# Batch 0's exchange through DRAM, the offset behind the last DFT, and small constants off the head of a queue

## The chip, the cores and the metric

The kernel runs on one core of a Trainium2 chip. The metric is the device time of one execution in microseconds (us); lower is better. Each kernel was run several times and the median is quoted. A difference of more than 2% counts as faster or slower, anything less as the same. Where a number comes from a profile it belongs to one profiled execution, whose span is about 2 us shorter than the time of the same execution.

## The reference

Eight batches of 3008 tokens by 256 channels go through a spectral mix and then through an expert:

```python
X = np.fft.rfft(x, axis=1)                       # x: (8, 3008, 256)
Yr = X.real @ w_r - X.imag @ w_i + b_r
Yi = X.real @ w_i + X.imag @ w_r + b_i
Yr = sign(Yr) * max(|Yr| - 0.01, 0); Yi likewise # soft shrinkage
y  = np.fft.irfft(Yr + 1j * Yi, n=3008, axis=1)

h = y.reshape(24064, 256) @ w_in                 # w_in: (256, 2048)
r = max(h, 0)
out = (s * r * r + b) @ w_out                    # w_out: (2048, 256)
```

## The kernel before

A transform of 3008 = 94 x 32 points is done in two steps, so there is a first DFT (94 rows in, 96 out), a middle one of 32 points, and on the way back a middle inverse and a last DFT. The middle stages work on "pairs", 24 a batch. Between the first DFT and the middle, and between the middle and the last, the data changes its layout. Batches 1 to 7 do that through DRAM: `u` is written to `ud` and fetched as `us`; `v` is written to `vd` and fetched as `vs`. Their stages are strewn over the expert tiles of the batch before, one unit in this or that slot (a slot is one of the 16 column blocks of the first expert matmul; a tile of 512 tokens has 16 slots).

Batch 0 has nothing to hide behind. So it keeps everything in SBUF and turns the layout by matmuls with an identity matrix:

```python
def inv_dft(ec, u):
    ps = other_bank()
    z = zt.pop((ec, u))
    for j in range(4):
        nc.tensor.matmul(ps[:, j * P : (j + 1) * P], z[:, j, :], T_t[:, 4 * u + j, :], start=True, stop=True)
    evac(vt[:, ec, :, 16 * u : 16 * u + 16], ps.rearrange("p (k n) -> p n k", n=N2), 512)

def turn(ec, k):                                  # line 435
    ps = two_banks()
    for j in range(8):
        nc.tensor.matmul(ps[0:96, j // 4, (j % 4) * P : (j % 4) * P + P],
                         vt[:, ec, 8 * k + j, :], eye_t, start=True, stop=True)
    h, n = divmod(8 * k, HW)
    evac(vs[(0, h)][:, n : n + 8, ec * P : (ec + 1) * P], ps[0:96].rearrange(...), 1024)
```

(The profile calls the matmul engine, TensorE, PE, and its weight loads PEld; POOL is GpSimd and SP is SyncE, which both issue transfers.) `evac` copies PSUM to SBUF on VectorE (DVE) or ScalarE (ACT), whichever has less work. The schedule of what follows:

```python
more = first_batch()
schedule(0, 8, more)                              # rest of batch 1's first DFT
plan.setdefault(17, []).append(lambda: emit_load_x(2))
...                                               # cut: scaling of w_out, bias
schedule(14, 20, corr_units())                    # the offset that soft shrinkage adds, built on DVE
schedule(30, 42, s23_units(1))                    # middle stages of batch 1, slots 30 to 72
schedule(82, 12, s4_units(1))                     # last DFT of batch 1
```

Of the kernel before, what the change touches and what calls it, by code (L numbers as in the profile page):

```python
# [14 lines left out]
P = 128  # L15
# [57 lines left out]
def _offset_rows(inv):  # L73

    v = inv.reshape(2, 2, N2, NPAIR, 2, N2).sum(axis=2)
    return v.transpose(0, 1, 3, 4, 2).reshape(2, P, NPAIR)


def _tile_order(nb):


    tiles = []
    rest = []
    for b in range(nb):
        tiles += [("main", b, j, 512) for j in range(5)]
        pr, half = divmod(b, 2)
        if pr == 0:
            rest.append(("tail", 0, 448 * half, 448))
        elif half == 1:
            rest += [("tail", pr, 0, 512), ("tail", pr, 512, 384)]  # L90
        if rest:
            tiles.append(rest.pop(0))
    return tiles + rest


@with_exitstack
def kernel(
# [20 lines left out]
    YSCALE = 1.0 / (N * VSCALE)  # L118
# [4 lines left out]


    ones_r, ones_i = _offset_rows(inv)
    real_row = np.zeros((P, 1), bool)
    real_row[[0, 64]] = True
    assert np.abs(np.where(real_row, ones_i, ones_r)).max() < 1e-9
    O_d = nc.inline_tensor(
        np.where(real_row, ones_r, ones_i).astype(np.float32), name="offset_rows"  # L130
    ).ap()
    A_d = nc.inline_tensor(first.astype(np.float16), name="dft_first").ap()
    F_d = nc.inline_tensor(fwd.astype(np.float16), name="dft_fwd").ap()
    T_d = nc.inline_tensor(inv.astype(np.float16), name="dft_inv").ap()
    C_d = nc.inline_tensor(last.astype(np.float16), name="dft_last").ap()
# [4 lines left out]
    E_d = nc.inline_tensor(np.eye(P).astype(np.float16), name="identity").ap()  # L140
# [7 lines left out]
    xpool = ctx.enter_context(tc.tile_pool(name="xp", bufs=5))  # L148
    upool = ctx.enter_context(tc.tile_pool(name="up", bufs=2))
# [59 lines left out]
    F_c = uspool.tile([P, NPAIR, 2, N2], F16, name="F_c", tag="us")  # L209
    nc.sync.dma_start(out=F_c.rearrange("p q r k -> p q (r k)"), in_=F_d)  # L210
# [3 lines left out]
    for r in (0, 64):  # L214
        for i, bv in enumerate((b_r, b_i)):
            nc.sync.dma_start(out=b_g[r : r + 1, i], in_=bv.unsqueeze(0))
    b_h = cpool.tile([P, D], F16, name="b_h")
# [5 lines left out]
    eye_t = cpool.tile([P, P], F16, name="eye_t")  # L223
    nc.sync.dma_start(out=eye_t, in_=E_d)
# [8 lines left out]
    o_t = cpool.tile([P, NPAIR], F32, name="o_t")  # L233
    nc.sync.dma_start(out=o_t, in_=O_d)
    bl = cpool.tile([P, D], F32, name="bl")
    nc.sync.dma_start(out=bl, in_=b_i.unsqueeze(0).to_broadcast([P, D]))
    for r in (0, 64):
        nc.sync.dma_start(out=bl[r : r + 1], in_=b_r.unsqueeze(0))
# [6 lines left out]
    for dc in range(DC):  # L245

        nc.gpsimd.tensor_copy(out=w_in_t[dc][0:1, 0:1], in_=T_c[0:1, 0, 0:1])
        nc.gpsimd.dma_start(out=w_in_t[dc], in_=moe_w_in[dc * P : (dc + 1) * P, :])
# [21 lines left out]
    F_2 = [uspool.tile([P, H, P], F16, name="F_2", tag="us") for _ in range(2)]  # L270
    for f in F_2:
        nc.vector.memset(f, 0.0)

    nc.vector.memset(b_h, 0.0)
    nc.vector.tensor_copy(out=b_h[0:1], in_=b_g[0:1, 0])
    nc.vector.tensor_copy(out=b_h[64:65], in_=b_g[64:65, 1])
# [10 lines left out]
    def place_tables():  # L287
        for i in range(2):
            nc.scalar.copy(out=W_t[:, :, i], in_=w_st[i])
        for a in range(2):  # L290
            r = slice(64 * a, 64 * a + 64)
            nc.vector.tensor_copy(out=blocks(F_t)[r, :, :, a], in_=F_c[r])

            for h, f in enumerate(F_2):
                q = slice(h * H, h * H + H)
                nc.vector.tensor_scalar_mul(
                    out=blocks(f)[r, :, 0, a], in0=F_c[r, q, 1], scalar1=-1.0
                )
                nc.vector.tensor_copy(out=blocks(f)[r, :, 1, a], in_=F_c[r, q, 0])
        for i in range(4):  # L300
            r = slice(32 * i, 32 * i + 32)
            c = 64 * (i % 2)
            nc.scalar.copy(out=T_t[r, :, c : c + 64], in_=T_c[r])  # L303

    cs = []
    sq_last = [None]

    def scale_w_out(q):
        st = wo_st[q]
        if not cs:  # L310
            cs.append(other_bank())
        wb = zpool.tile([P, 2, D], F16, name="wb", tag="z")
        with tc.issue_after(sq_last[0].ins):
            nc.vector.tensor_scalar_mul(
                out=w_out_t[:, 2 * q : 2 * q + 2, :], in0=st, scalar1=s_bc
            )
            nc.vector.tensor_scalar_mul(out=wb, in0=st, scalar1=bb_bc)
        load["dve"] += 0.8
        for j in range(2):
            nc.tensor.matmul(  # L320
                cs[0][:, 0:D], ones, wb[:, j],
                start=(q == 0 and j == 0), stop=(q == MC // 2 - 1 and j == 1),
            )
# [8 lines left out]
    def first_batch():  # L332
# [20 lines left out]
        with tc.issue_after(last_dve.ins), tc.issue_after(last_act.ins):  # L353
            place_tables()
        emit_load_x(1)
        for q in range(MC // 2):
            emit_load_w_out(q)


        U = NPAIR // 4  # L360
        vt = bigpool.tile([P, DC, N2, 96], F16, name="vt", tag="corr")
        gs = {}
        zt = {}
        g_last = [None]

        def mix(ec, u):
            ps = two_banks().rearrange("p h (j r e) -> p (h j) r e", j=2, r=2)
            for j in range(4):
                q = 4 * u + j
                for dc in range(DC):  # L370
                    nc.tensor.matmul(
                        ps[:, j], ut[:, dc, 4 * q : 4 * q + 4, :],
                        W_t[:, dc, :, ec * P : (ec + 1) * P],
                        start=(dc == 0), stop=(dc == DC - 1),
                    )
            g = vpool.tile([P, 4, 2, P], F16, name="g0", tag="v")
            if u % 3 == 1:
                nc.scalar.copy(out=g, in_=ps)
                load["act"] += 1.02
            else:  # L380
                g_last[0] = nc.vector.tensor_tensor(
                    out=g, in0=ps,
                    in1=b_g[:, :, ec * P : (ec + 1) * P].unsqueeze(1).to_broadcast([P, 4, 2, P]),
                    op=ALU.add,
                )
                load["dve"] += 1.2
            gs[(ec, u)] = g

        def fwd_dft(ec, u):
            ps = one_bank().rearrange("p (j e) -> p j e", j=4)  # L390
            g = gs.pop((ec, u))
            seeded = u % 3 == 1
            if seeded:
                nc.tensor.matmul(
                    ps, sel_t,
                    b_h[:, ec * P : (ec + 1) * P].unsqueeze(1).to_broadcast([P, 4, P]),
                    start=True, stop=False, skip_group_check=True,
                )
            for j in range(4):
                q = 4 * u + j  # L400
                for r, f in enumerate((F_t[:, q, :], F_2[q // H][:, q % H, :])):
                    nc.tensor.matmul(
                        ps[:, j, :], f, g[:, j, r, :], start=(r == 0 and not seeded),
                        stop=(r == 1), skip_group_check=seeded,
                    )
            pos = mpool.tile([P, 4, P], F32, name="m", tag="m")
            nc.scalar.activation(out=pos, in_=ps, func=AF.Relu, bias=neg_lam)
            z = zpool.tile([P, 4, P], F16, name="z", tag="z")
# [5 lines left out]
            zt[(ec, u)] = z  # L414

        def inv_dft(ec, u):
            ps = other_bank()
            z = zt.pop((ec, u))
            for j in range(4):
                nc.tensor.matmul(  # L420
                    ps[:, j * P : (j + 1) * P], z[:, j, :], T_t[:, 4 * u + j, :],
                    start=True, stop=True,
                )
            evac(
                vt[:, ec, :, 16 * u : 16 * u + 16],
                ps.rearrange("p (k n) -> p n k", n=N2), 512,
            )

        for h in range(2):
            vs[(0, h)] = vspool.tile([96, HW, D], F16, name="vs", tag="vs")  # L430

        def turn(ec, k):
            ps = two_banks()
            for j in range(8):
                nc.tensor.matmul(
                    ps[0:96, j // 4, (j % 4) * P : (j % 4) * P + P],
                    vt[:, ec, 8 * k + j, :], eye_t, start=True, stop=True,
                )
            h, n = divmod(8 * k, HW)
            evac(  # L440
                vs[(0, h)][:, n : n + 8, ec * P : (ec + 1) * P],
                ps[0:96].rearrange("p h (j e) -> p (h j) e", e=P), 1024,
            )

        last = s4_units(0)
        more = s1_units(1)

        def some(n):
            for _ in range(n):
                if more:  # L450
                    more.pop(0)()

        steps = [(ec, u) for ec in range(DC) for u in range(U)]
        for i in range(2 * U + 2):
            if i < 2 * U:
                mix(*steps[i])
            if 0 <= i - 1 < 2 * U:
                fwd_dft(*steps[i - 1])
            if 0 <= i - 2 < 2 * U:
                inv_dft(*steps[i - 2])  # L460
            k = i - U - 2
            if 0 <= k < 4:
                turn(0, k)
            if 0 <= k - 1 < 4:
                last.pop(0)()
                last.pop(0)()
            if i >= 2 * U:
                some(3)
            if i == 6:
                with tc.issue_after(g_last[0].ins):  # L470
# [365 lines left out]
```

## Time and profile before

| | before |
|---|---|
| median of three runs | 900.83 us (899.37 to 901.06) |
| span of the profiled run | 900.1 us |
| mean granted clock of TensorE (share of full speed) | 0.991 |
| PE, DVE, ACT busy | 96%, 72%, 70% |
| first matmul of the expert stage (line 674) | 61.2 us |
| from there to the end | 838.9 us |

The last two rows: a *head* up to the first expert matmul and a *rest* behind it.

What the transfers do while the old exchange runs is in the windows of 5 us (after the window and its length come busy time and instructions of PE, its weight loads, DVE, ACT and POOL, then the granted clock, the share of the DMA engines, GB/s):

```profile
45.00:50.00 5.00, 4.33 (x67) 3.86 (x65) 4.77 (x8) 4.42 (x8) 0.00 (x0) 1.00 0.02 5
55.00:60.00 5.00, 3.73 (x49) 2.60 (x47) 2.75 (x4) 4.30 (x6) 0.51 (x1) 1.00 0.96 194
```

From 40 to 55 us the DMA engines are idle: the turns are on PE, and no transfer is on the path.

### The profile page before, as it was taken

The numbers are of one execution on the slowest core, as the hardware profiler recorded it, in microseconds if no ns is written. First come the engines' busy times: TensorE is split into PE (matmuls) and PEld (weight loads), VectorE is DVE, ScalarE is ACT, GpSimd is POOL, SyncE is SP. The second block draws the span as 40 slices with busy tenths as digits, with TensorE's granted clock in tenths as the row PEclk, the third lists the DMA queues.
The fourth block names the chain that finished last, engine by engine and source line by source line (L and its number), as shares of the span: only waits on it lengthen the run. The fifth ranks groups of instructions, "written<-read, shape, count | busy, mean of one in ns | idle before, by whom it ended". The sixth has DMA issues, their size and how long they took to land.

```text
span 900.1 us, 16484 instructions
## 1 busy us (share of the span) xinstructions
PE 861.8 (96%) x6748; PEld 610.8 (68%) x6748; DVE 652.4 (72%) x870; ACT 631.6 (70%) x785; POOL 33.2 (4%) x58
## 2 busy tenths in 40 slices
PE   2989998999999999999999999999999999999997
PEld 2756765767767676677767776777767777766665
DVE  4779776677678767777778677777767777676664
ACT  2879776667776677767776767777777676776662
POOL 2310000000000000000000000000000000000000
PEclk9989999899999999999999999999999999999999
DMA  8735146512365117612465115631254121411111
GB/s 183 188 75 148 47 109 154 148 33 59 86 184 129 57 48 185 178 36 60 88 181 131 57 36 139 163 92 54 65 155 132 36 62 47 118 41 36 36 36 53
DMA packets 81407, 86.91 MB, mean 97 GB/s; under 512 B 5422, under 2 KB 73268, under 8 KB 79988
## 3 DMA queue, kind: packets, MB, share of 16 engines
q1 hardware_dynamic: 76820, 70.39, 26.5%
q0 software_dynamic: 4512, 15.47, 10.3%
q8 instruction: 53, 0.87, 0.4%
q14 instruction: 22, 0.18, 0.1%
HBM read 52.55 MB, written 46.66 MB: 110 GB/s over the span
## 4 chain that ended last, share of the span: by engine, by line
PE 83%; ACT 6%; DMA 5%; DVE 4%; issue 1%; SPq 1%; DVEq 0%; ACTq 0%
PE psh L674 33%; PE psa L735 33%; PE psf L562 7%; PE psf L495 3%; ACT rt L681 2%; PE psf L633 2%; PE psf L544 2%; PE psf L580 2%; DMA ud<-u 2%; DMA T_c<-dft_inv 2%; DVE gt L688 1%; DMA vs<-vd 1%; ACT T_t L303 1%; DVE m L568 1%; ACT gt L685 1%
## 5 line engine op out<-in xcount | busy, mean ns | idle before, releaser
L681 ACT ACTIVATE rt<-psh 128x1024 f32<-128x1024 f32 (+2 forms) x384 | 385.4, 1005 | 176.4 <-PE psh L674 175.4
L735 PE MATMUL psa<-w_out_t,gt 128*128 128x256 f16 x3024 | 456.3, 273 | 0.0
L688 DVE TENSOR_TENSOR gt<-rt 128x1024 f16<-128x1024 f32 (+2 forms) x291 | 348.6, 1199 | 134.4 <-ACT rt L681 133.2
L735 PEld LDWEIGHTS <-gt 128*128 128x128 f16 x3024 | 295.4, 98 | 191.5 <-issue 7.0
L674 PE MATMUL psh<-yt,w_in 128*128 128x512 f16 x1280 | 382.0, 380 | 0.5 <-DVE yt L175 0.3
L674 PEld LDWEIGHTS <-w_in 128*128 128x128 f16 x1536 | 143.8, 98 | 26.8 <-issue 3.4
L685 ACT ACTIVATE gt<-rt 128x1024 f16<-128x1024 f32 (+1 forms) x93 | 98.1, 1055 | 2.5
L562 PE MATMUL psf<-W_t,xf 128*128 128x256 f16 x672 | 87.2, 273 | 0.0
L170 ACT CAST u<-psf 96x512 f16<-96x512 f32 x99 | 57.0, 578 | 26.6 <-PE psf L495 24.8
L748 DVE TENSOR_TENSOR ost<-psa,bias_bc 128x512 f32<-128x512 f32 (+2 forms) x98 | 65.1, 666 | 11.8 <-PE psa L735 8.8
L562 PEld LDWEIGHTS <-xf 128*128 128x128 f16 x672 | 65.5, 98 | 8.9 <-issue 0.4
L674 PE MATMUL psh<-tail,w_in 128*128 128x384 f16 (+2 forms) x256 | 70.3, 356 | 0.0
L568 DVE TENSOR_TENSOR m<-psf,lamb 128x512 f32<-128x512 f32 x84 | 57.6, 686 | 9.7 <-PE psf L562 9.7
L587 DVE TENSOR_TENSOR v<-psf,corr 128x512 f16<-128x512 f32 x84 | 57.0, 682 | 6.9 <-PE psf L580 6.8
L570 DVE SCALAR_TENSOR_TENSOR z<-psf,m 128x512 f16<-128x512 f32 x84 | 58.0, 690 | 2.5
L170 ACT CAST xf<-psf 128x512 f16<-128x512 f32 x84 | 48.7, 579 | 13.2 <-PE psf L544 13.1
L171 ACT ACTIVATE yt<-psf 128x480 f16<-128x480 f32 (+2 forms) x73 | 37.7, 536 | 16.2 <-PE psf L633 16.0
L495 PE MATMUL psf<-x,A_t 94*96 94x512 f16 x112 | 44.2, 394 | 3.7 <-DVE z L570 1.4
L550 DVE TENSOR_SCALAR xf<-xf 128x256 f16<-128x256 f16 x84 | 18.2, 222 | 36.5 <-ACT xf L170 36.5
L633 PE MATMUL psf<-C_t,vs 96*128 96x96 f16 x480 | 37.2, 209 | 7.2 <-DMA vs<-vd 4.3
L633 PEld LDWEIGHTS <-vs 96*128 96x128 f16 x512 | 33.1, 100 | 12.1 <-DMA vs<-vd 4.6
L194 POOL DMA_DIRECT2D x<-in_x_dram x32 | 16.7, 524 | 480.4 <-PE psf L495 471.0
(66 smaller groups left out, 343.0 us busy)
## 6 DMA issues: line engine op xcount, KB each, us to landing
out_dram<-ost SPq DMA_DIRECT2D x160, 128.0 KB
x<-in_x_dram POOLq DMA_DIRECT2D x32, 376.0 KB, 6.2
ud<-u SPq DMA_DIRECT2D x28, 384.0 KB
us<-ud SPq DMA_DIRECT2D x28, 384.0 KB
vd<-v SPq DMA_DIRECT2D x42, 256.0 KB
vs<-vd SPq DMA_DIRECT2D x14, 768.0 KB
wo_st<-in_moe_w_out_dram POOLq DMA_DIRECT2D x8, 256.0 KB, 4.8
out_dram<-ost SPq DMA_DIRECT2D x16, 112.0 KB
```

The costliest lines, as they stand in the source:

```text
L170: return None, nc.scalar.copy(out=dst, in_=src)
L495: nc.tensor.matmul(ps[0:96, :], A_t[0:N1, :], x16[(b, c)][0:N1, j * D : (j + 2) * D], start=True, stop=True,)
L562: nc.tensor.matmul(ps[:, j, :], xt[:, j * DC + dc, lo : lo + P], W_t[:, dc, w], start=(m == 0 and dc == 0), stop=(m == 1 and dc == DC - 1),)
L568: nc.vector.tensor_tensor(out=m, in0=ps, in1=lamb, op=ALU.max)
L570: nc.vector.scalar_tensor_tensor(out=z, in0=ps, scalar=2 * LAM, in1=m, op0=ALU.add, op1=ALU.min)
L633: nc.tensor.matmul(ps[:, j * 96 : (j + 1) * 96], vs[(b, h)][:, k, ec * P : (ec + 1) * P], C_t, start=True, stop=True,)
L674: nc.tensor.matmul(o, w_in_t[dc][:, mc * P : (mc + 1) * P], r, start=(dc == 0), stop=(dc == DC - 1),)
L681: nc.scalar.activation(out=rt[:, :, 0:w], in_=ps[:, :, 0:w], func=AF.Relu)
L685: nc.scalar.activation(out=gt[:, :, 0:w], in_=rt[:, :, 0:w], func=AF.Square)
L688: sq_last[0] = nc.vector.tensor_tensor(out=gt[:, :, 0:w], in0=rt[:, :, 0:w], in1=rt[:, :, 0:w], op=ALU.mult)
L735: nc.tensor.matmul(ps[0:n, h, :], gts[(ti, mc // 2)][:, mc % 2, sub * P : sub * P + n], w_out_t[:, mc, :], start=(mc == 0), stop=(mc == MC ...
L748: nc.vector.tensor_tensor(out=ost[0:m, lo:hi], in0=ps[0:m, lo:hi], in1=bias_bc[0:m, lo:hi], op=ALU.add,)
```

## The change

Four intents. Batch 0's exchange goes through DRAM as in the other batches, in groups of pairs while the mix runs, so that 64 matmuls and 8 large evictions go. The casts of the bias and the placing of the table T_t move on DVE behind the first eviction of the mix, and the loads of the bias ahead of a large table, so that nothing waits at DVE's head. The offset is added as one signal behind the last DFT, in place of a `corr` tile added to every `v`. And the middle stages of batch 1 run earlier.

```diff
+    vd = dpool.tile([NPAIR, P, D], F16, name="vd", tag="vd")
+    vd_rows = vd.rearrange("q (k n) e -> (q k) n e", n=N2)
 ...
-    def turn(ec, k): ...                     # 64 matmuls with the identity, 8 evictions
+        def inv_dft(i):
+            ...                              # two matmuls of 256 columns
+            v = xfpool.tile([P, 2 * DC * 192], F16, name="v0", tag="xf")   # three buffers
+            v = v[:, 0 : 2 * D].rearrange("p (j e) -> p j e", j=2)
+            evac(v, ps, 512)
+            nc.sync.dma_start(out=vd[2 * i : 2 * i + 2].rearrange("q p e -> p q e"), in_=v)
+        def fetch(k0, k1):
+            for h in range(2):
+                last[1] = nc.gpsimd.dma_start(
+                    out=vs[(0, h)][k0:k1], in_=vd_rows[k0:k1, h * HW : (h + 1) * HW, :])
 ...                                         # cut: the loop over i = 0 to 13, whose last lines are
+            if i in (5, 9):
+                fetch(8 * (i - 5), 8 * (i - 1))
+        fetch(64, 96)
+        with tc.issue_after(last[1].ins):
+            emit_load_raw()                  # w_out once more, for the bias: 2 MB read
+        for u in s1_units(1, True):          # first DFT of batch 1, all 16 units
+            u()
 ...
+    def place_t():                           # called behind the first eviction of the mix, on DVE
+        nc.vector.tensor_copy(out=b_h[0:1], in_=b_g[0:1, 0])
+        nc.vector.tensor_copy(out=b_h[64:65], in_=b_g[64:65, 1])
+        for i in range(4): ...               # T_t, was nc.scalar.copy
 ...
-            nc.vector.tensor_tensor(out=v[...], in0=ps, in1=corr[0][...], op=ALU.add)
+            evac(v[:, h : h + 2, :], ps, 512)
 ...
+            nc.vector.scalar_tensor_tensor(  # last DFT of batches 1 to 7
+                out=yt[:, ec, n2 : n2 + w, :], in0=off[0][:, n2 : n2 + w, :],
+                scalar=bl[:, 1, ec : ec + 1], in1=ps[...], op0=ALU.mult, op1=ALU.add)
 ...
-    schedule(30, 42, s23_units(1))
+    schedule(16, 44, s23_units(1))
+    plan.setdefault(17, []).append(emit_load_next)   # x of batch 2
+    plan.setdefault(30, []).append(emit_load_off)    # 1.5 MB, the offset signal
```

Also: four x buffers for five, three `u` buffers for two, loads of x of batch 1 and w_out behind a gate (an instruction that waits for earlier data and that the loads have to follow), the scale of the last DFT in its table, and tiles of another shape ("wide") for batches 0 and 1.

## The prediction

> **What bounds the kernel now.** I read the page first, parts 1 and 2.
>
> ```profile
> PE 861.8 (96%) x6748; PEld 610.8 (68%) x6748; DVE 652.4 (72%) x870; ACT 631.6 (70%) x785; POOL 33.2 (4%) x58
> PE   2989998999999999999999999999999999999997
> PEclk9989999899999999999999999999999999999999
> ```
>
> PE is busy nearly always, so I asked whether busy means full. By-shape counts of matmuls, at the spacing that the chain of waits shows (two 128x512 in 0.43 us, so 0.215 each; four 128x256 in 0.44, so 0.11), fill windows exactly: from 90 to 105 us 24 of 0.215, 81 of 0.11 and 12 small ones of about 0.08 make 15.0 us. From 68 us to 153 and from 163 to the end PE is the bound and nothing beside it matters. What can be won is the start (first matmul of the expert stage, line 674, at 61.4 us) and the two slices where PEclk reads 8. The waits of PE name what lies there:
>
> ```profile
> PE psh L340 <- DVE ut L174: 7.5, 3, 6.5
> PE psh L340 <- DMA x<-in_x_dram: 7.5, 2, 6.5
> PE psf L633 <- DMA vs<-vd: 4.3, 1, 4.3
> PE psf L633 <- DVE u L174: 1.8, 1, 1.8
> ```
>
> The second row is the load of x and mostly stays; the first and third are what I follow. The timeline of the head:
>
> ```profile
> 13.77 0.28 DVE L275 CAST b_h<-b_g 1x256 f16<-1x256 f32 x1 [5.36 <-DMA b_g<-in_b_r_dram]
> ...
> 16.25 1.44 PE L340 MATMUL psh<-A_t,x 94*128 94x96 f16 x16 [6.46 <-DVE ut L174]
> ...
> 21.37 1.14 ACT L289 CAST W_t<-w_st 128x512 f16<-128x512 f32 x2
> ...
> 22.41 5.91 ACT L303 COPY T_t<-T_c 32x1536 f16<-32x1536 f16 x4
> 22.56 3.57 PE L371 MATMUL psh<-W_t,ut 128*128 128x256 f16 x16 [1.60 <-ACT W_t L289]
> ```
>
> DVE stands in front of a 1x256 bias cast until a 1 KB load lands; behind it wait the evictions of the first DFT, and PE 6.46 us behind those. Then ACT spends 5.91 us placing T_t, which holds the first copies of the mix (the next ACT row is at 28.35). The third wait, by windows of 1 us (after the length: busy time of PE, its weight loads, DVE, ACT and POOL, then the granted clock, the DMA share and GB/s):
>
> ```profile
> 155.00:156.00 1.00, 0.00 (x0) 0.00 (x0) 0.17 (x1) 0.00 (x0) 0.00 (x0) 1.00 1.01 205
> 157.00:158.00 1.00, 0.19 (x3) 0.19 (x4) 0.00 (x0) 0.00 (x0) 0.00 (x0) 0.50 0.48 166
> 161.00:162.00 1.00, 1.00 (x7) 0.49 (x6) 0.00 (x0) 0.57 (x1) 0.00 (x0) 0.50 0.06 16
> 163.00:164.00 1.00, 1.00 (x15) 0.77 (x12) 0.86 (x2) 0.00 (x0) 0.00 (x0) 1.00 0.00 0
> ```
>
> PE has nothing from 153.5 to 157.8 (batch 1's exchange is still on its way) and then works at a granted clock of 0.50 until about 162.6: 4.3 us of idling and half of 4.8 us, together 6.7. The same happens from 60 to 68 us (mean clock 0.57, 8 x 0.43 = 3.4 us lost).
>
> **What the Trainium skill says.** "TensorE: Matmul & The Clock Gate", section "What's actually happening": the array's clock is halved after an idle window of about 3.4 us and comes back after about as long of work. The trace agrees: 4.3 us idle, then 0.50 for some 5 us. Same page, "Wait — 56ns, not 53.3ns?": warm matmuls start N/2.4 GHz + 2.5 ns apart, 215.7 ns at N = 512; the trace has 0.215. "DMA: Bandwidth & Descriptors", section "Anatomy of one DMA — SWDGE (gpsimd) path": about 2.0 us fixed for each DMA, mostly the write's receipt. The trace's smallest one (bb_bc, 0.5 KB) took 2.11 us. Same page, "Issuing engines are not separate DMA queues": all queues share 16 engines. The trace agrees: T_c, 384 KB behind the loads of x, needed 14.5 us.
>
> **The change part by part.** *Head.* The bias cast leaves DVE's head: the 6.46 us wait becomes a wait for x. Chunk 0 lands at 6.5, chunk 1 at 9.0, so one comes each 2.5 us (estimate) and chunk 3 at 13.9, a little earlier since the fifth and sixth x chunk no longer load in between (four buffers, and a gate): 13.6. Its two groups need about 1.9 us to the last eviction (20.2 to 22.1 before), W_t follows: mix starts at 16.6 in place of 22.6, **6 us earlier**. place_f on DVE ends near 18.5. T_t moves to DVE, 4 copies at the 0.55 us of the like F_t copy, plus two bias casts of 0.28: 2.8 us, behind the first eviction of the mix, in place of 5.9 on ACT.
>
> *Mix loop.* PE work is the same, 12 steps of 8 x 0.11 + 8 x 0.056 + 4 x 0.056 + a third of 0.215, i.e. 1.6 us, 19 us in all. DVE has 8 x 1.22 (g) + 12 x 0.69 (z) + 2 evictions x 0.69 + 2.8 + 0.6 (lamb) = 22.8 us and is the slower one. In the old loop (30.1 to 51.6) DVE was 85% busy. After the first z, near 23.7 by these durations (30.1 before), 17.4 us remain; at 0.85 to 0.9 that is 20, so the last z ends at **43.5**.
>
> *Exchange.* The 64 transposing matmuls of line 435 (64 x 0.056 = 3.6 us of PE) and 8 evictions of 1.0 to 1.2 us go. In place come 12 writes and 6 fetches. The first two groups of pairs hide in the loop; the last does not: inverse DFT and eviction 0.9, issue 0.4, write 2.1 or a bit more, two fetches issued by POOL 1.0, landing 2.3. So vs is whole at **50.3**. Batch 1's first DFT fills this time: 16 evictions of 0.58 or 0.68 on two engines take 5 us, so PE has a gap of 2 to 3 us, near the clock gate's window; I count 0.5 us for it. The last DFT is 64 matmuls of about 0.085 (5.5 us): the expert stage starts at about **56.5**, in place of 61.4, and without the 6 matmuls of line 495 (1.3 us) and 13 of line 633 (1.0 us) that it carried along before.
>
> *First tile.* Before it was over at 75.0: 13.6 us, of which 3.0 to 3.4 were the low clock and 2.3 those leftovers. Now PE has 32 x 0.215 + 16 x 0.11 = 8.6 us, but ACT and DVE have 8 x 1.02 (rt) + 8 x 1.2 (gt) + 8 x 0.48 (w_out_t, the second scaling wb is gone) = 21.6, half of it 10.8 us. It ends at 67.3: **7.7 us won**. From here PE is the bound again; 6 of the 16 ones-matmuls were still open at 75.0 before, 0.65 us more.
>
> *Schedule of batch 1.* Its middle stages run in slots 16 to 60 in place of 30 to 72, and the last DFT still starts at slot 82. The exchange that took 10.5 us then has 22 slots of over 1.1 us in place of 10: the wait and the low clock behind it go, **6.7 us won**.
>
> *The rest.* The offset leaves DVE's v (84 x 0.68) for a plain eviction on either engine; line 633's evictions (in batches 1 to 7: 69 on ACT, 29 on DVE) all become one DVE instruction of about 0.65. The corr tile (24, 7.5 us) and wb (3.8 us) go. The sum of ACT and DVE hardly moves, and both are at 70%; hidden. The wide tiles have the same matmul count (6 tiles a batch, 16 x 2 + 16 x 4 each). Sum: 7.7 + 6.7 - 0.65 = 13.8, and 1.5, a guess, for the relief of DVE from 74 to 90 us (16.00 of 16 busy there): **900.8 - 15.3 = 885.5 us.**
>
> **The rivals.** (a) *The DRAM round trip takes the place of the transposes in full.* Write and fetch share the engines with w_out (2 MB) and x; the two exchanges seen took 5.5 us (ud) and 10.5 us (vs). If the last group needs 10 us rather than 6, and PE goes cold behind it, 4 + 2.5 us come back: 891. For it: all w_out loads stand before the fetch in POOL's queue. Against: the last group is a third of the bytes, and loads were over by 40 us before.
> (b) *DVE becomes the bound in the last DFTs:* 14 instructions of 0.65 in 12 slots, with squares of 1.2 in the same queue and two psf banks. A slot has about 1.4 us of PE work there; DVE 0.76 for these, 0.1 for stores, leaving room for half the squares. I expect under 0.5 us a batch; at 1 us times 7 it would be 892.
> (c) *The new load w_raw is late:* it starts behind the last fetch near 50 us, 2 MB of fp32 reads; w_in, as large, took 7 to 8.5 us, twice that when sharing with ud and us. It is wanted at the end of the first tile, 66. A stall of 0 to 3 us.
> (d) *The loop runs at PE's pace, not DVE's* (19 us), and the clock stays up: 3 to 4 us better, 881.
>
> **Range and chances.** Parts (a) to (c) push up by 3 to 7 us each with chances of a fifth to a third, (d) down by 4 with a quarter. 8 in 10 lie between 879 and 893. Faster by over 2% means under 882.8, which takes (d) and none of the others: 0.28. Slower by over 2% would take a new stall of 33 us: 0.01. Within 2%: 0.71.
>
> **What would show it.** Mix's first matmul at 16 to 18 us with no DVE wait before b_g; T_t on DVE; last z at 42 to 45; PE's wait for vs of batch 0 under 4 us; first expert matmul at 54 to 59; no PE wait for vs near 150 us and PEclk 1.00 there; PE waits on DVE yt of a few us at most. The prediction is wrong if PE is cold for more than one stretch in the head, if w_raw stalls PE at slot 15, or if the last DFTs of batches 1 to 7 show new gaps.

## More of the kernel before

The turns and the last DFT of the first 128 channels lie beside the middle stages of the second 128, and units of batch 1's first DFT fill the holes.

The head is read from the summary of line 674, whose columns are the shortest, median and longest duration in ns, and then the first and last start in us:

```profile
L674 PE MATMUL psh<-yt,w_in x1280: 376/379/631, 61.2 to 861.1; 128*128 128x512 f16 x183
```

## The result, and the profile after

The changed kernel took **896.14 us** (895.87 to 898.63, four runs), beside 900.94 for the kernel before (four runs). The ratio is 0.9956, 95% interval 0.9935 to 0.9977: the same, by the 2% rule, and 10.6 us more than predicted. (A ratio here is the mean time of one kernel's fast runs over that of the other's of the same rounds, so not quite the ratio of the quoted medians.)

Parts 1 and 2 of the page:

```profile
PE 856.0 (96%) x6564; PEld 607.0 (68%) x6564; DVE 652.8 (73%) x842; ACT 616.3 (69%) x776; POOL 35.1 (4%) x65
PE   4777999999999999999999999999999999999996
PEclk9978999999999999999999999999999999999999
```

Against the page before, the first slice of PE is better (4 for 2), but slices 2 to 4 are worse (777 for 989); the low clock at slice 8 is gone, while slice 3, low already, reads 7 for 8, and slice 4 reads 8 for 9. The waits of PE (total us, times, longest) say by whom:

```profile
PE psf L539 <- DMA us<-ud: 5.0, 1, 5.0
PE psh L479 <- DMA vs<-vd: 4.7, 1, 4.7
PE psa L426 <- DVE z L415: 4.4, 4, 2.4
```

The wait for `vs` of batch 1 near 157 us has gone, but a wait for `vs` of batch 0, one for `us` of batch 1 and one inside the mix loop have come. Rows of the timeline (start, duration, engine, line, what; in brackets the idle time before and what ended it):

```profile
17.23 3.45 PE L379 MATMUL psh<-W_t,ut 128*128 128x512 f16 x8 [1.60 <-ACT W_t L282]
...
33.23 0.59 ACT L171 CAST v<-psa 128x512 f16<-128x512 f32 x1 [3.43 <-DMA vd<-v]
...
51.12 0.97 POOL L438 DMA_DIRECT2D vs<-vd  x2 [5.48 <-DMA vd<-v]
53.26 2.08 POOL L195 DMA_DIRECT2D x<-in_x_dram  x4
56.94 0.80 PE L479 MATMUL psh<-C_t,vs 96*128 96x96 f16 x8 [4.67 <-DMA vs<-vd]
78.00 0.61 PE L539 MATMUL psf<-F_t,us 128*128 128x128 f16 x4 [5.00 <-DMA us<-ud]
```

The mix starts at 17.23 in place of 22.56, as intended. Then ACT stands 3.4 us before an eviction of `v`, because all three buffers hold writes to `vd` that have not landed; the last two fetches are issued from 51.12 on and the last DFT starts at 56.94, when the first of them, half of `vs`, has landed. (The second landed at 58.28, before PE came to its half.) Windows, in the columns explained above:

```profile
20.00:25.00 5.00, 3.87 (x21) 2.00 (x20) 4.88 (x10) 2.88 (x4) 0.00 (x0) 1.00 1.05 211
25.00:30.00 5.00, 4.89 (x31) 2.94 (x31) 3.92 (x5) 3.85 (x6) 4.81 (x8) 1.00 1.05 217
55.00:60.00 5.00, 3.06 (x39) 3.10 (x40) 1.91 (x2) 1.49 (x4) 0.90 (x2) 0.50 1.02 247
60.00:65.00 5.00, 5.00 (x36) 3.07 (x33) 1.99 (x4) 2.92 (x5) 0.00 (x0) 0.52 1.36 220
75.00:80.00 5.00, 2.00 (x10) 1.25 (x11) 0.31 (x2) 1.36 (x2) 0.00 (x0) 0.50 1.08 309
155.00:160.00 5.00, 4.80 (x46) 3.28 (x44) 5.00 (x9) 3.21 (x4) 0.00 (x0) 1.00 0.27 88
```

In the first five of these, in which something is late, the DMA share is 1.0 or more; before the change it was 0.02 while the exchange ran. Behind two of the waits the clock is 0.50. And the last row is the gain: PE busy and the clock 1.00 where both were low before. The first expert matmul:

```profile
L681 PE MATMUL psh<-yt,w_in x1344: 363/379/634, 62.0 to 854.6; 128*128 128x512 f16 x174, 128*128 128x480 f16 x18
```

So the head is 62.0 us where it was 61.2 and 56.5 was predicted, and the rest is 832.1 where it was 838.9. For the prediction the rest is 885.5 - 1.8 - 56.5 = 827.2 (1.8 is the difference of time and span in the changed kernel's profiled run). The miss is 5.5 us in the head and 4.9 in the rest.

### The profile page after: what moved, and what is told of

Read it like the earlier page. It is cut to its first block, busy times and chain, and to the rows that moved or that the text cites. A ratio compares the mean times of both kernels' runs of the same rounds, so it can differ in the third digit from the quotient of the medians.

```text
span 894.1 us, 16087 instructions
## 1 busy us (share of the span) xinstructions
PE 856.0 (96%) x6564; PEld 607.0 (68%) x6564; DVE 652.8 (73%) x842; ACT 616.3 (69%) x776; POOL 35.1 (4%) x65
## 4 chain that ended last, share of the span: by engine, by line
PE 78%; issue 10%; DMA 5%; DVE 3%; ACT 2%; POOL 0%; SPq 0%; POOLq 0%; ACTq 0%
PE psa L750 32%; PE psh L681 31%; PE psf L557 7%; DMA x<-in_x_dram 4%; PE psf L623 2%; PE psf L507 2%; PE psf L539 2%; PE psf L575 2%; DMA vd<-v 1%; ACT rt L688 1%; DVE gt L695 1%; DVE yt L628 0%; DVE g L389 0%; SPq L734 0%; PE psh L379 0%
## 5 line engine op out<-in xcount | busy, mean ns | idle before, releaser
L695 DVE TENSOR_TENSOR gt<-rt 128x1024 f16<-128x1024 f32 (+2 forms) x301 | 363.4, 1209 | 144.2 <-ACT rt L688 141.4
L750 PE MATMUL psa<-w_out_t,gt 128*128 128x256 f16 (+1 forms) x3024 | 458.0, 273 | 0.0
L750 PEld LDWEIGHTS <-gt 128*128 128x128 f16 (+1 forms) x3024 | 300.6, 101 | 182.3 <-issue 2.5
L681 PE MATMUL psh<-yt,w_in 128*128 128x512 f16 (+1 forms) x1344 | 399.9, 380 | 0.0
L692 ACT ACTIVATE gt<-rt 128x1024 f16<-128x1024 f32 (+2 forms) x83 | 84.7, 1021 | 1.8
L760 DVE TENSOR_TENSOR ost<-psa,bias_bc 128x512 f32<-128x512 f32 (+1 forms) x96 | 65.1, 678 | 26.1 <-PE psa L750 23.8
L628 DVE SCALAR_TENSOR_TENSOR yt<-off,bl,psf 128x480 f16<-128x480 f32 (+1 forms) x98 | 62.0, 666 | 7.8 <-PE psf L623 6.6
L565 DVE SCALAR_TENSOR_TENSOR z<-psf,m 128x512 f16<-128x512 f32 x84 | 58.1, 691 | 2.8
L171 ACT CAST v<-psf 128x512 f16<-128x512 f32 x83 | 48.1, 580 | 17.1 <-PE psf L575 16.1
L681 PE MATMUL psh<-tail,w_in 128*128 128x512 f16 (+1 forms) x192 | 53.2, 352 | 0.0
L539 PE MATMUL psf<-F_t,us 128*128 128x128 f16 x336 | 32.9, 221 | 5.0 <-DMA us<-ud 5.0
```

The source lines that it names most:

```text
L171: return None, nc.scalar.copy(out=dst, in_=src)
L565: nc.vector.scalar_tensor_tensor(out=z, in0=ps, scalar=2 * LAM, in1=m, op0=ALU.add, op1=ALU.min)
L628: nc.vector.scalar_tensor_tensor(out=yt[:, ec, n2 : n2 + w, :], in0=off[0][:, n2 : n2 + w, :], scalar=bl[:, 1, ec : ec + 1], in1=ps[:, 0 : ...
L681: nc.tensor.matmul(o, w_in_t[dc][:, mc * P : (mc + 1) * P], r, start=(dc == 0), stop=(dc == DC - 1),)
L692: nc.scalar.activation(out=gt[:, :, 0:w], in_=rt[:, :, 0:w], func=AF.Square)
L695: sq_last[0] = nc.vector.tensor_tensor(out=gt[:, :, 0:w], in0=rt[:, :, 0:w], in1=rt[:, :, 0:w], op=ALU.mult)
```

## The experiments

**Theory A:** the transfers share 16 DMA engines. Large loads and stores that are in flight (x, w_in, w_out, then w_raw, x of batch 2, the offset signal and batch 1's own `ud`) stretch the small exchanges on the path; with three `v` buffers a stretched write becomes a stall of the loop, and each long wait brings half a clock behind it. **Theory B:** the DRAM exchange has a fixed latency, or an order in its queue, that no lighter traffic would shorten. Twelve kernels were run, all with correct results. They ran in four sets, each beside runs of the kernel before on the same chip (medians 900.79, 898.96, 901.61 and 901.14), so kernels of different sets are compared by their ratios or by their profiles.

### e1: the loads of x(2) and of the offset wait until us(1) is in

```diff
+            if hold is not None:
+                nc.gpsimd.tensor_copy(out=t[0:1, 0:1], in_=hold)
-            emit_load_x(2)
+            emit_load_x(2, us[(1, 3)][0:1, 5, 0:1])
+            nc.gpsimd.tensor_copy(out=off[0][0:1, 0, 0:1], in_=us[(1, 3)][0:1, 5, 0:1])
```

> The changed kernel (896.1 us), where the loads of x for batch 2 and of the offset signal (4.6 MB of reads and SBUF writes) now wait until batch 1's own data (us) has landed. Theory A, shared DMA engines: these loads were in flight from 53 to 77 us and stretched the small exchange of batch 1 (ud, us), so PE's 5.0 us wait for us near 75 us and the half clock behind it (3.5 us) go: 887 to 890 us. The 4.7 us wait for vs stays, since w_raw still stands directly behind the last fetch. Theory B, the round trip's own latency and the order of the queues: us comes as late as before, 895 to 897 us.

The added copies are of one element: each waits for `us` of batch 1, and the load has to follow it.

Measured: 892.78 us (889.89 to 895.37), ratio 0.9908 (0.987 to 0.9946). The wait for `us` is gone, so theory A holds for that one: the rest falls from 832.1 to 825.7 us. The wait for `vs` stays, and the head becomes 63.5:

```profile
PE psh L481 <- DMA vs<-vd: 5.7, 1, 5.7
```

So x(2) and the offset were what delayed `us`, and not what delays `vs`.

### e2: e1, and the load of w_raw waits too

```diff
+        nc.gpsimd.tensor_copy(out=w_raw[0][0:1, 0, 0:1], in_=us[(1, 3)][0:1, 5, 0:1])
-    plan.setdefault(15, []).append(make_bias)
+    plan.setdefault(22, []).append(make_bias)
```

(Not shown: batch 1's first DFT now stands ahead of the load of w_raw in the program.)

> As the run before, and w_raw (2 MB of reads) waits for us too; the bias is made at slot 22 in place of 15. Theory A: the last fetch of vs meets only the ud stores, lands 2 to 3 us after its issue in place of 5, PE's wait for vs falls from 4.7 to 2 to 3 us and the clock stays up behind it: 3 to 6 us under the run before, 882 to 886 us. Theory B: the wait for vs stays above 4 us and the time within 1 us of the run before. Risk in both: w_raw comes late for slot 22 and PE waits there.

Measured: 897.84 us (896.77 to 899.38), ratio 0.9966. A miss:

```profile
PE psa L325 <- DMA w_raw<-in_moe_w_out_dram: 6.2, 1, 6.2
PE psh L480 <- DMA vs<-vd: 5.5, 1, 5.5
```

The `vs` wait is 5.5 us although neither w_raw nor x(2) nor the offset is in flight then, so none of them is its cause; and the gated w_raw comes so late that PE waits 6.2 us for it. What is left beside the fetch is batch 1's own stores to `ud`, 1.5 MB, for which e7 was made.

### e3: the kernel before, with the middle stages of batch 1 in slots 22 to 66

```diff
-    schedule(30, 42, s23_units(1))
+    schedule(22, 44, s23_units(1))
```

> The kernel before (900.9 us), with one line changed: batch 1's middle stages in slots 22 to 66 in place of 30 to 72. Both theories: PE's 4.3 us wait for vs near 155 us and the half clock behind it go, 6.7 us: 893 to 895 us. If it stays above 898, the gain that the changed kernel shows at that place is not the schedule's.

Measured: 894.31 us (893.44 to 895.19), ratio 0.9926 (0.9898 to 0.9954). A change of two numbers in one line gains as much as the whole change. The window in which the kernel before idled and ran at half clock:

```profile
155.00:160.00 5.00, 5.00 (x58) 3.82 (x56) 3.91 (x5) 3.98 (x7) 0.51 (x1) 1.00 0.43 45
```

PE is busy for all of it, at full clock.

### e4: the kernel before, with the bias casts behind the tables

```diff
-    nc.vector.tensor_copy(out=b_h[0:1], in_=b_g[0:1, 0])
-    nc.vector.tensor_copy(out=b_h[64:65], in_=b_g[64:65, 1])
 ...
             place_tables()
+            nc.vector.tensor_copy(out=b_h[0:1], in_=b_g[0:1, 0])
+            nc.vector.tensor_copy(out=b_h[64:65], in_=b_g[64:65, 1])
```

> The kernel before, with one thing changed: the two bias casts (b_h) stand behind the placing of the tables on DVE, as in the changed kernel. The mix starts 5 to 6 us earlier (17 in place of 22.6 us); if nothing behind it takes the gain: 895 to 896 us. If the loads that come behind (x of batch 1, w_in, w_out) hold the head instead, less: 898 to 900.

Measured: 899.02 us (897.86 to 900.24), ratio 0.9974 (0.994 to 1.0008). A miss: the mix starts at 17.46 as it should, but ACT's 5.9 us of T_t (18.58 to 24.5) stand ahead of its first copy of the mix, which comes at 24.51. The head is 59.0, only 2.2 us better. The gain at the head needs T_t off ACT as well, which the change does and this kernel did not.

### e6: the kernel before with all the small parts, and the turns kept

From the change: late bias casts, T_t on DVE, bias loads first, the buffer counts, the gate; and slots 22 to 66. Not from it: the DRAM exchange, w_raw, the moved offset, the wide tiles.

```diff
-pool "xp" bufs=5, "up" bufs=2
+pool "xp" bufs=4, "up" bufs=3
+    def place_t(): ...                       # bias casts, then T_t with nc.vector.tensor_copy
+            if i == 0:
+                with tc.issue_after(g_last[0].ins):
+                    place_t()
+        with tc.issue_after(gate.ins):
+            emit_load_x(1); ...
-    schedule(30, 42, s23_units(1))
+    schedule(22, 44, s23_units(1))
```

> The kernel before with every part of the change except the exchange through DRAM, the offset and the wide tiles: bias casts and T_t behind the first mix on DVE, bias loads ahead of the DFT table, x with four buffers and behind a gate, three u buffers, batch 1's middle stages earlier. Batch 0 is still turned by matmuls. Theory A (the exchange through DRAM is what eats the head's gain): mix starts near 17.3 us, the expert stage near 55, 882 to 887 us, i.e. below the changed kernel (896.1) and below the gated one (892.8). Theory B (the loads of the head hold the start whatever the exchange): expert stage not before 58 us, 889 to 893 us.

Measured: **885.36 us** (885.08 to 886.57), ratio 0.9847 (0.9816 to 0.9877). The head:

```profile
L680 PE MATMUL psh<-yt,w_in x1280: 376/379/390, 53.5 to 844.5; 128*128 128x512 f16 x183
```

53.5 us, 8.5 less than in the changed kernel, with the same early start of the mix; and the granted clock is 1.00 in every window from 15 to 90 us. So the early start is worth its 6 us and more if the exchange stays on PE. That points to the DRAM exchange as what ate it; e10, which keeps the other parts of the change, tests that.

### e7: e2, with batch 1's first DFT and its stores behind the last DFT of batch 0

```diff
-        for u in s1_units(1, True):
-            u()
         yt = yts[0] = ypool.tile(...)        # last DFT of batch 0
 ...
+        for u in s1_units(1, True):
+            u()
```

> A measurement, not an improvement: the gated kernel with w_raw gated too, and batch 1's first DFT with its ud stores behind the last DFT of batch 0, so nothing but the last pairs' writes and fetches is on the DMA engines then. Theory A (sharing): from the issue of the last two fetches to the first matmul of the last DFT 3.5 to 4.3 us in place of the 6.4 to 6.6 us of the two gated runs. Theory B (the round trip's own latency): 5.5 us or more.

One look, 900.88 us, of unknown state; it is slow by design, since batch 1's first DFT is now on the path. What it is for:

```profile
52.06 0.97 POOL L441 DMA_DIRECT2D vs<-vd  x2 [5.91 <-DMA vd<-v]
55.54 0.80 PE L476 MATMUL psh<-C_t,vs 96*128 96x96 f16 x8 [6.60 <-DMA vs<-vd]
```

From the issue of the last two fetches to the first matmul: 3.5 us, of which 1.0 is the issue. The same stretch is 5.8 us in the changed kernel, 6.6 in e1 and 6.4 in e2. That is theory A, and against B, which had 5.5 or more. It is one look, though, and e7 also takes the evictions of batch 1's first DFT out of the stretch. The other traces help, for the stretch varies: in e13 below, whose head has the same code as the changed kernel, it was 4.0, with those evictions beside it. What goes with it is how many of the four stores of `ud` (384 KB each) were issued before the fetch. From the issue of the first of the two fetches to its landing it took 3.3 us with none (e7), 3.9 and 4.0 with one (e13, e9), and with two 5.0 (e8), 5.7 (the changed kernel) and 6.1 to 6.5 (e1, e2, e11, e12). That is an order found in the traces, not an edit that was tried.

### e8: e1, with seven free buffers for v in place of three

```diff
-            v = xfpool.tile([P, 2 * DC * 192], F16, name="v0", tag="xf")
+            v = gpool.tile([P, 2, 512], F16, name="v0", tag="gt")
```

> The first gated kernel (892.8 us), with seven buffers for the outgoing v of batch 0 in place of three. Its ACT waited 3.4 us near 30 us for a v buffer whose write to DRAM took 8.7 us. If the buffers are what turns slow writes into a stall: the wait goes, the mix ends 2 to 3 us earlier and the time falls to 889.5 to 891. If the last fetch is bound by the DMA engines anyway, the wait for vs grows by what the mix gains: 892 to 893.

Measured: **885.83 us** (885.19 to 886.92), ratio 0.985 (0.9824 to 0.9875), more than I had expected. ACT's wait for the write is gone, and the whole chain behind it moves:

```profile
47.83 0.97 POOL L440 DMA_DIRECT2D vs<-vd  x2 [6.20 <-DMA vd<-v]
...
52.98 0.80 PE L481 MATMUL psh<-C_t,vs 96*128 96x96 f16 x8 [3.83 <-DMA vs<-vd]
```

The fetch is issued 4.1 us earlier than in e1 (51.88) and lands faster (5.1 us for 6.6), so the head is 58.1 for 63.5. The DMA share is still 1.03 to 1.07 from 20 to 35 us, but no eviction waits for a write. One thing came with the edit: the evictions stand in another order on ACT, the first of them at 29.94 us (24.31 in the changed kernel), so the first write is issued at 30.55 and not at 24.92. e11 and e12 have that order too. How much is the buffers' and how much the later writes', no run parts.

### e9: e1, with 24 useless matmuls to keep the clock up

```diff
+        warm = one_bank()
+        with tc.issue_after(s1_mm[0].ins):
+            for k in range(24):
+                nc.tensor.matmul(warm, ones, w_in_t[0][:, 0:512], start=True, stop=True)
```

> The first gated kernel with 24 useless matmuls of 512 columns (5.2 us) on PE in the wait for vs. It takes no wait away; it keeps PE from idling. If the half clock behind the wait costs what the trace suggests (from 57 to 65 us, 6.5 us of work at half speed), 2.5 to 3.5 us come back: 889 to 890.5 us. If the clock is not the cause, 892 to 894.

Measured: 897.3 us (894.31 to 897.69), ratio 0.9969, above both ranges. Inconclusive in time, because the schedule came out differently: batch 1's first middle matmul stood ahead of the expert tile and PE waited 5.9 us for `us`. But it measures one thing by itself: with the clock at 1.00 the 64 matmuls of the last DFT took 3.25 us (61.20 to 64.45), where the changed kernel, at 0.50, took 5.28 (56.94 to 62.22).

### e10: the changed kernel, with only batch 0's exchange undone

Turns, the scheme of the last DFT in batch 0 and the bias from scaled copies as before; the moved offset, wide tiles and early slots as in the change; loads gated as in e1.

```diff
-        def inv_dft(i): ... evac(v, ps, 512); nc.sync.dma_start(out=vd[...], in_=v)
-        def fetch(k0, k1): ...
+        def inv_dft(ec, u): ... evac(vt[...], ..., 512)
+        def turn(ec, k): ...                 # as in the kernel before
-    def make_bias(): ... w_raw ...
+            nc.vector.tensor_scalar_mul(out=wb, in0=st, scalar1=bb_bc)
```

> The changed kernel with only batch 0's exchange undone: transposes on PE as before the change, the bias from the scaled copies as before, offset behind the last DFT, wide tiles and the earlier middle stages of batch 1 as in the changed kernel, x(2) and the offset load held until us(1) is in. Theory A (the shared transfers around the DRAM exchange ate the head's gain, the rest of the change is worth what the steady part showed: batch 2's copy to the end 2.4 us shorter than in e3): 885.4 - 2.4 = 883, between 881 and 885, clock 1.00 in every window from 15 to 90 us, no PE wait over 2 us behind the load of x. Theory B (the exchange through DRAM costs a fixed latency that the transposes do not, nothing else): the same time here, so this run does not separate A from B; it separates both from theory C, that the offset's new place and the wide tiles cost something in the steady part, which would put it above 887.

Measured: **880.69 us** (880.49 to 882.02), ratio 0.9774 (0.9758 to 0.979): faster by over 2%, the best of all kernels here, and a little below the range that I gave. The clock row of its page and its first expert matmul:

```profile
PEclk9999999999999999999999999999999999999999
...
L715 PE MATMUL psh<-yt,w_in x1344: 363/379/382, 53.1 to 839.9; 128*128 128x512 f16 x174, 128*128 128x480 f16 x18
```

A head of 53.1 and a rest of 825.6, with no PE wait over 1.6 us behind the load of x. Theory C, that the moved offset and the wide tiles cost something, falls: the rest was 829.9 in e6, which has neither of them, so they cost nothing that shows; with the gates and the earlier slots they win some 4 us. As the DRAM exchange is what e10 takes out of e1, with the new bias, the 892.78 of e1 and its head of 63.5 against 880.69 and 53.1 say what that exchange cost with three buffers.

### e11: e8, with the bias from scaled copies, so without the 2 MB load

> e8 (DRAM exchange, seven free v buffers, x(2) and the offset load held) with the bias from the scaled copies on DVE as before the change, so that the 2 MB load of w_raw is gone. Theory A: the fetch no longer shares with w_raw and PE's 1.8 us wait for it goes, but DVE does 16 scalings more in the first tile (about 3.8 us beside PE): 882 to 885, vs wait 3.5 us or less. If w_raw was harmless: 886, as e8.

Measured: 884.86 us (884.57 to 885.58), ratio 0.9817 (0.9802 to 0.9831), within the range. But the detail was a miss: the wait for `vs` did not shrink, it was 5.1 us, and from the issue of the fetch to the first matmul it was 6.2 us (48.13 to 54.33) with nothing large in flight but `ud`. So w_raw is not what stretches it, as in e2. The edit is the bias part of e10's. Since e11 ran beside e10 and differs from it only in the exchange and in the order of work and the tables' layout that go with it, the pair is the cleanest price of that exchange at its best, with buffers and loads mended: 884.86 - 880.69 = 4.2 us.

### e12: the changed kernel with the seven v buffers and nothing else

> The changed kernel with batch 0's v tiles in a pool with seven free buffers in place of three, and nothing else. If the stall of the loop and the loads that reach into the first tile are two separate losses (they added up from 896 over 893 to 886 when taken in the other order): ACT's 3.4 us wait for the write of v gone, last inverse matmul near 44, span 3 to 5 us shorter than the changed kernel, 891 to 893, and PE's wait for us(1) still there, 4 us or more. If they are one loss that either cure removes: 887 or less with the us wait gone, or no gain, 895 to 897, with the vs wait as much longer.

Measured: 892.73 us (892.1 to 893.85), ratio 0.9904 (0.9883 to 0.9925), as expected of two separate losses. The waits of PE:

```profile
PE psh L479 <- DMA vs<-vd: 5.4, 1, 5.4
PE psf L539 <- DMA us<-ud: 4.8, 1, 4.8
```

The last pair of inverse matmuls starts at 43.93 (46.95 in the changed kernel) and the head is 59.8, but the wait for `us` is untouched and the rest is still 832.3.

### e13: the changed kernel with the late slots of batch 1's middle stages

```diff
-    schedule(16, 44, s23_units(1))
+    schedule(30, 42, s23_units(1))
```

> The changed kernel with only the new slots of batch 1's middle stages undone (30 to 72 again). If the slots are what the change's net gain comes from, as e3 says: the PE wait for vs(1) of about 4 us and the clock of 0.50 are back near 155 us, about 6 us longer, 901 to 903, so no gain over the kernel before. If the moved offset and the wide tiles had removed that wait in another way: 896 to 897.

Measured: 894.91 us (893.45 to 899.0), ratio 0.9937 (0.9908 to 0.9967). Neither expectation holds, and my reading of e3, that the slots are what the net gain comes from, falls with it. Two waits and a window:

```profile
PE psa L322 <- DMA w_raw<-in_moe_w_out_dram: 2.6, 1, 2.6
PE psf L623 <- DMA vs<-vd: 2.0, 1, 2.0
...
155.00:160.00 5.00, 5.00 (x38) 3.20 (x37) 3.58 (x7) 2.02 (x3) 0.00 (x0) 0.66 0.50 162
```

The wait for `vs` of batch 1 is back, smaller (2.0 us, and a clock of 0.66 for 5 us, which costs 5 x 0.34 = 1.7). But the 5.0 us wait for `us` is gone, and with it the low clock behind that. The early slots ask for `us` at slot 16, and in the changed kernel it has not landed then. This profile has a loss of its own, a wait of 2.6 us for w_raw (0.2 in the changed kernel) with the clock at 0.50 from 66.4 to 69.8, so the two profiles can't be set off wait by wait. In the medians, moving the middle stages forward inside the changed kernel bought one wait with another and won nothing that shows (0.9937 without it, 0.9956 with it); it wins only where `us` is in early enough, as in e1, e3 and e10.

### All in one table

| kernel | median, us | ratio to before | head | rest |
|---|---|---|---|---|
| before | 900.94 | 1 | 61.2 | 838.9 |
| prediction | 885.5 | | 56.5 | 827.2 |
| changed | 896.14 | 0.9956 | 62.0 | 832.1 |
| e13 late slots | 894.91 | 0.9937 | 62.0 | 831.5 |
| e1 loads gated | 892.78 | 0.9908 | 63.5 | 825.7 |
| e12 v buffers | 892.73 | 0.9904 | 59.8 | 832.3 |
| e8 both | 885.83 | 0.985 | 58.1 | 826.0 |
| e11 both, no w_raw | 884.86 | 0.9817 | 59.4 | 824.4 |
| e3 before, slots | 894.31 | 0.9926 | 60.0 | 832.2 |
| e6 before, small parts and slots | 885.36 | 0.9847 | 53.5 | 829.9 |
| e10 changed, turns on PE | 880.69 | 0.9774 | 53.1 | 825.6 |
| e2 gated, w_raw too | 897.84 | 0.9966 | 63.0 | 832.3 |
| e4 before, late bias casts | 899.02 | 0.9974 | 59.0 | 839.1 |
| e7 fetch alone (one look) | 900.88 | | 61.9 | 837.2 |
| e9 e1 with useless matmuls | 897.3 | 0.9969 | 70.4 | 825.5 |

Head and rest are of the profiled run. Gating acts on the rest (824 to 826 with it, 832 without, and 832 in e2, where PE waits for w_raw), the buffers and the turns on the head, and the two add up. In kernels with turns (before, e3, e6, e10) some matmuls of the last DFT and of batch 1's first DFT still stand behind the first expert matmul, which makes their head look somewhat better and their rest worse; the medians have no such bias.

## Why the prediction was wrong

Three steps failed: the mix loop, in which a wait for a buffer was missing (3.4 us); the exchange, sized for idle DMA engines (6.8 us predicted, 10.0 measured); and the schedule of batch 1, in which the earlier stages met a new wait for `us` (5.0 us, and 1.9 lost to the low clock behind it), which took back the 6.7 won. The start of the mix, T_t and the first tile were right.

*Head: right up to the loop.* The mix started at 17.23 (16.6 predicted), T_t took 2.25 us on DVE and DVE waits for no bias. e4 and e6 show that both moves were needed.

*Mix loop: wrong.* The last `z` was put at 43.5 and ended at 46.9 (46.21 + 0.69). I had counted engine time only; the missing 3.4 us are ACT's wait of 3.43 us for a buffer. The first write to `vd` was issued at 24.92, and its buffer was free for the eviction at 33.23, 8.3 us later, where I had set 2.1 "or a bit more" for a write and had not asked how many buffers stand behind it. Three buffers at one write each 2 us cover about 6 us. e12 gives seven, the wait goes, and the last inverse matmuls come 3 us earlier; that is shown for the edit as a whole, with its other order on ACT (see e8). What stretched the write is not tested: by the trace, the loads of x of batch 1 and of w_out were in flight from 25 to 32 us, which is the traffic that rival (a) names.

*Exchange: this is the term that was mis-sized.* From the last `z` to the whole `vs` I had 6.8 us; it took 10.0 to the first half, with which PE can start (46.9 to 56.9), and 11.4 to the second. Of the parts, the inverse, the eviction and the write were near their sizes (the fetch was issued at 51.12, 4.2 us behind the last `z`, for 3.4 in the sum), but from the end of the issue to the first use it took 4.85 us for 2.3. In e7, where nothing else was in flight, that was 2.5: my figure was the one for an idle set of engines. Rival (a) had this mechanism, with the loads of w_out in the first place; I gave it a fifth to a third, and argued against it that "loads were over by 40 us before". That was a reading of the old kernel's traffic, and the change put four new transfers there. Which traffic does it is shown for `us` (x(2) and the offset, e1) and excluded for `vs` (not w_raw, not x(2): e2 and e11). That it is `ud` rests on e7, and on the order in nine traces that is given there: the more of `ud` was issued ahead of the fetch, the longer it took. Also, the sum of rival (a) should read 892 (885.5 + 6.5), not 891.

*The clock.* I counted 0.5 us; the last DFT ran wholly at 0.50. I took a gap of 2 to 3 us to be near the limit, but in the kernel before, the clock had fallen at 60.4 us in a wait of only 1.8. It cost 5.28 - 3.25 = 2.0 us by e9's measure. As I had put 5.5 us for these 64 matmuls at full clock, where 3.25 is right, the two errors hid each other, by luck: from `vs` to the first expert matmul I had 6.2 us, and it took 5.1. So the sum of the head is 3.4 + 3.2 - 1.1 = 5.5 us, the miss in the table.

*First tile: right.* 10.8 us predicted; PE ran from 62.0 to its wait at 73.0. Rival (c), a late w_raw, did not stall the changed kernel at its slot (0.2 us), but it cost PE waits of 1.0, 1.8 and 2.6 us in e1, e8 and e13.

*Schedule of batch 1: wrong by a missing question.* The wait at 157 us went, as I said, and 6.7 us with it. I did not ask what the moved stages need at slot 16: `us`. Its first fetch is issued only at 62.8 us, when `ud` has landed, and beside x(2), w_raw and the offset. Then the third of its four fetches holds SyncE for 10.0 us (the row gives the shortest, median and longest issue in ns, then the first and last start in us):

```profile
L521 SPq DMA_DIRECT2D us<-ud x4: 377/931/10022, 62.8 to 73.9; - x4
```

So the fourth is issued at 73.9. In e1 the first goes out as late (62.5) but all four are issued by 67.4. A late head is not the reason: e12 has it 2.2 us earlier and waits 4.8. PE waits 5.0 us for it from 73.0 to 78.0 and runs at 0.50 until about 81.9, which is half of 3.9 us more: some 6.9 lost for 6.7 won. e13 undoes the slots and loses nothing in the median; e1 takes the loads away and wins 6.4 in the rest, which is then 825.7, 1.5 better than my sum. So this wait is the whole miss of 4.9 in the rest, and the other terms there were a little low; no run parts them.

*Rivals (b) and (d).* DVE did not become the bound in the last DFTs: PE's waits behind 90 us are all 0.5 us or less. A time of 881 us was there, but not by a loop at PE's pace: e10 has it with the exchange on PE. What the transposing matmuls cost, 3.6 us of PE and eight evictions, was the wrong thing to weigh. They lie beside other work, at full clock, while the last part of the exchange that replaced them lay open in every kernel here that has it.

The prediction's citations hold, with two limits: the clock needed some 5 us of work to come back behind the wait of 4.3 us, where it cites 3.4 (see the list at the end), and bb_bc, whose 2.11 us it sets beside the page's 2.0 for GpSimd's path, is issued by SyncE. On the shared engines the page "DMA: Bandwidth & Descriptors" of the Trainium skill has more, which I should have drawn on: its section "Queues, rings and completion order" says that each engine goes round between the rows it has work for, packet by packet. So a small fetch shares with whatever other rows hold. The runs agree in effect: the fetch of 256 KB pieces took 3.5 us from issue to use with nothing beside it and 5.1 to 6.6 beside two or more stores of `ud`, which were issued by another engine. No run shows the packets' order itself.

## What to carry to other kernels

Price a transfer on the path by the traffic that the *changed* program has in flight at that moment, not by its duration alone or by the old trace's idle engines, and give its source as many buffers as its stretched duration takes. When a stage is moved earlier, list what it reads and when that lands. And before a busy-looking piece of PE work is replaced by a round trip, ask whether it was on the path: in e6 and e10, with the turns on PE, the clock was 1.00 from 25 to 90 us, and in the changed kernel it was 0.50 for 17 us of that.

## What the Trainium skill lacked or had wrong

- "DMA: Bandwidth & Descriptors", section "Anatomy of one DMA — SWDGE (gpsimd) path", gives about 2.0 us and the bytes over 436 GB/s for one DMA. For an undisturbed fetch the runs are somewhat above it (e7: 256 KB landed 3.3 us behind the start of its issue, 2.6 by our estimate from that formula). The formula has no term for other traffic. In windows with the DMA share at 1.0 or more, the load of the 1.5 MB offset signal, 5.6 us by our estimate from it, took 22.1 us from issue to landing, and w_raw (2 MB), 6.8 by it, took 13.4. A write of 128 KB, which SyncE issued, held its buffer for 8.3 us.
- The same page says that DMAs of all issuing engines interleave, and gives no figure for what a small transfer pays. Here the last fetch of batch 0 took from 3.5 us (alone, e7) to 6.4 us (beside 1.5 MB of stores, e2), and the issue of one fetch held SyncE for 10.0 us.
- "TensorE: Matmul & The Clock Gate", section "What's actually happening", has the clock halved after an idle window of about 3.4 us. Here it fell 2.0 to 2.5 us after PE's last matmul (at 156.0 us before the change, at 54.6 and 75.0 after it), and at 60.4 us before the change although PE had been busy for 1.87 of the 3.41 us before.
- The same section has the full clock back after about 3.4 us of sustained work. Behind the wait that ended at 78.0 us it was so: 0.50 until about 81.9. Behind the waits for `vs` of batch 0, with the same 64 matmuls of 96 columns first, it took 4.0 us (e2), 5.1 (e12), 5.3 (e11), 6.4 (e8), 6.9 (e1) and 7.9 (the changed kernel, 56.94 to 64.8). The section says that the window runs freely, from which we estimate up to two windows, 6.8 us; the 7.9 is well beyond that, and why, no run here shows.
